# Row maximum of the attention scores through a difference of keys: pairs 0 to 7 beside the MLP, with ScalarE's relu and a fourth PSUM bank

## Chip, cores and metric

One core of one Trainium2 chip runs the whole program. The metric is the device time of one execution in microseconds (us); lower is better. The five engines of the core are called PE (TensorE, matmuls), DVE (VectorE), ACT (ScalarE), POOL (GpSimd) and SP (SyncE, which here only issues DMAs); PEld is PE's weight load. Each engine works through its own instructions in their order.

## The reference

S = 2048 tokens, D = 640 channels, 32 heads of width 20, MLP width F = 1728, all in fp32:

```python
g = sigmoid((x * gate_w).sum(-1, keepdims=True))
q, k, v = heads of x @ wqkv
a = softmax(q @ k.T * 20 ** -0.5) @ v  -> heads joined -> @ wo
h = layernorm(x)                        # over the channels
u = gelu(h.T @ w1 + b1)                 # over the tokens: (D, S) @ (S, F)
b = (u @ w2 + b2).T
out = g * a + (1 - g) * b
```

The softmax is made stable with the maximum of each query's 2048 scores. The change touches how that maximum is found, and when.

## The kernel before

**Layout.** The 32 heads are taken as 16 pairs. fp32 products are made from a rounded part and a rest ("hi" and "lo", helper `hi_lo`): q is stored twice in DRAM (`q_d[0]` hi, `q_d[1]` lo), and so is k (`k_d`). A "stack" of a pair (`load_stack`, L95 on) puts 60 rows per head into one tile: hi, hi and lo of k against hi, lo and hi of q, so that one matmul of 60 rows gives a score tile in full precision. Head j of a pair sits at partition 64 j, so the matmuls of the two heads use different row groups of PE and run beside each other.

**Stages.** First PE makes q, k, v and the gate (`qk_unit`, L213, is one 128x512 piece: 15 matmuls, then ACT takes hi and DVE lo out of PSUM, and two DMAs store them). Then comes the MLP (`mlp`), then the attention loop, then the output projection.

**The maximum pass.** `s_tiles` (L168) makes for each pair, half of the queries, tile t of 128 queries and chunk kc of 512 keys the scores of both heads, j = 1 and then j = 0: one matmul (L178) into a PSUM tile of tag "s" (3 banks, taken in turn), and one DVE `tensor_reduce` with max (L180) of 128x512 into a column of `mx`. That is 128 tiles for a pair and 2048 in all. After each half, `s_max` and `s_store` take the maximum over the four chunks, negate it, split it and store it; the attention loop later loads it as two extra rows of q (`load_m`), so that its own matmul gives score minus maximum.

**Where the pass is put.** The pass is a generator; `s_next` emits one tile. PE's order is written out by hand. In the MLP, every step (`pair64`, L46: two matmuls of 64 rows, one in each row group) is followed by as many pairs of score tiles as an even spread of `S_AHEAD = 736` tiles over all 2592 steps asks for. So 5 pairs and three quarters are done there. The MLP has four PSUM banks of tag "st" of its own, and its results leave PSUM through ACT (L440, L452, L477); ACT also makes the hi parts of weights (L38), and POOL the lo parts (L41). The eighth PSUM bank, tag "pv", is used in the attention loop alone.

**The attention loop** has 512 iterations (16 pairs, 2 halves of the queries, 16 key tiles). Each has four matmuls of scores (L700, tag "st"), four exponentials on ACT (L703, 128x512 each), and eight matmuls with v into the bank "pv" (L637). Between the four score matmuls stand up to three tiles of the maximum pass, spread evenly: `due = (n + 1) * LEFT // 484 + 1` with `LEFT = 2048 - S_AHEAD`, and `take = min(due - given, 3)` in iteration n. With 1312 tiles left this gives 344 iterations with three, 140 with two and the last 28 with none.

**Loading the stacks.** In the MLP the stack of the next pair is put on a list (`drip`) when a pair starts, and one of its DMAs (18 for a pair) is issued on SP's queue at every second opportunity between score tiles. SP's queue carries the MLP's weights, too. The very first stack is loaded by POOL. In the loop, `s_stack` loads pair by pair on SP.

Of the kernel before, what the change touches and what calls it, by code (L numbers as in the profile page):

```python
# [7 lines left out]
F32 = mybir.dt.float32  # L8
F32R = mybir.dt.float32r
AF = mybir.ActivationFunctionType  # L10
OP = mybir.AluOpType
AX = mybir.AxisListType

P = 128
S, D, H, DH, F = 2048, 640, 32, 20, 1728
NP = H // 2
NT = S // P
NC = D // P
FF = 13
FT = 14  # L20
TL = F - FF * P
HALF = D // 2
VW = DH + 1
# [5 lines left out]
def gated_mix(ctx, tc, xT, x, wqk, wv0, wv1, wo, w1, w1t, b1, w2, b2, out):  # L29
    nc = tc.nc  # L30
# [5 lines left out]
    def hi_lo(hi, lo, src, hi_eng=None, lo_eng=None):  # L36
        if hi_eng is nc.scalar:
            nc.scalar.activation(hi, src, AF.Copy)  # L38
        else:
            (hi_eng or nc.vector).tensor_copy(hi, src)  # L40
        (lo_eng or nc.vector).tensor_sub(lo, src, hi.bitcast(F32))  # L41
# [12 lines left out]
    dram = ctx.enter_context(tc.tile_pool(name="dram", bufs=1, space=bass.MemoryType.DRAM))  # L54
    q_d = dram.tile([2, D, S], F32, name="q_d")
    k_d = dram.tile([2, D, S], F32, name="k_d")
    m_d = dram.tile([NP, 2, P, 32], F32, name="m_d")
    o_d = dram.tile([D, S], F32, name="o_d")
    l_d = dram.tile([H, S], F32, name="l_d")
# [4 lines left out]
    cp = ctx.enter_context(tc.tile_pool(name="cp", bufs=1))  # L64
    base = ctx.enter_context(tc.tile_pool(name="base", bufs=1))
    psum = ctx.enter_context(tc.tile_pool(name="psum", bufs=1, space=PSUM))
# [4 lines left out]
    def s_tile(shape, name):  # L71
        return psum.tile(shape, F32, tag="s", bufs=3, name=name)
# [12 lines left out]
    nc.gpsimd.memset(eps_t, EPS)  # L85
    b1_t = cp.tile([P, FT], F32, name="b1_t")
    b2_t = cp.tile([P, NT], F32, name="b2_t")
# [8 lines left out]
    drip = []  # L96

    def load_stack(p, ks, qs, full, eng=nc.sync):
        put = eng.dma_start if eng else lambda *a: drip.append(lambda: nc.sync.dma_start(*a))
        for j in range(2):  # L100
            r0 = 64 * j
            h = 2 * p + j
            rows = slice(DH * h, DH * h + DH)
            kf = ks.bitcast(F32)
            put(kf[r0: r0 + DH, :], k_d[0, rows, :])
            put(kf[r0 + DH: r0 + 2 * DH, :], k_d[0, rows, :])
            put(kf[r0 + 2 * DH: r0 + 3 * DH, :], k_d[1, rows, :])
            if full:
                put(kf[r0 + 3 * DH: r0 + 3 * DH + 2, :], ones)
            for i in range(2):  # L110
                qf = qs[i].bitcast(F32)
                cols = slice(i * (S // 2), (i + 1) * (S // 2))
                put(qf[r0: r0 + DH, :], q_d[0, rows, cols])
                put(qf[r0 + DH: r0 + 2 * DH, :], q_d[1, rows, cols])
                put(qf[r0 + 2 * DH: r0 + 3 * DH, :], q_d[0, rows, cols])
# [15 lines left out]
    s_src, st_src, v_tiles = {}, {}, {}  # L131
# [8 lines left out]
    def s_max(p, half, mx):  # L140
        mm = cp.tile([P, 16], F32, tag="mm", bufs=2, name=f"mm{p}_{half}")
        mc = cp.tile([P, 32], F32R, tag="mc", bufs=2, name=f"mc{p}_{half}")
        nc.vector.tensor_reduce(mm, mx.rearrange("p k j t -> p (j t) k"), axis=AX.X, op=OP.max)
        nc.gpsimd.tensor_scalar_mul(mm, mm, -1.0)
        hi_lo(mc[:, :16], mc[:, 16:], mm, hi_eng=nc.gpsimd, lo_eng=nc.gpsimd)
        s_close.append([8, lambda: s_store(p, half, mc)])
# [16 lines left out]
    def s_finish():  # L163
        next(stream, None)
        while s_close:
            s_close.pop(0)[1]()

    def s_tiles(p):  # L168
        for half in range(2):
            mx = cp.tile([P, 4, 2, 8], F32, tag="mx", bufs=2, name=f"mx{p}_{half}")  # L170
            for t in range(8):
                for kc in range(4):
                    for j in (1, 0):
                        def f(j=j, kc=kc, t=t):
                            ks, qs = s_src[p]
                            ps = s_tile([P, 512], f"s{p}_{half}_{t}_{j}_{kc}")
                            r = slice(64 * j, 64 * j + 3 * DH)
                            nc.tensor.matmul(ps, qs[half][r, t * P:(t + 1) * P], ks[r, kc * 512:(kc + 1) * 512],  # L178
                                             start=True, stop=True)
                            nc.vector.tensor_reduce(mx[:, kc, j, t: t + 1], ps, axis=AX.X, op=OP.max)  # L180
                        yield f
            s_close.append([2, lambda p=p, half=half, mx=mx: s_max(p, half, mx)])

# [10 lines left out]
    p1 = p1s.enter_context(tc.tile_pool(name="p1", bufs=1, side="right"))  # L194
# [13 lines left out]
        hi_lo(wh, wl, raw, hi_eng=nc.scalar)  # L208
        return wh, wl

    accs = iter(range(1000))

    def qk_unit(m, w, q):  # L213
        wh, wl = w
        ps = st_tile([P, 512], f"qk{m}_{q}")
        mm3(ps, [(wh[:, c], wl[:, c], xh[c][q], xl[c][q]) for c in range(NC)])
        hi = p1.tile([P, 512], F32R, tag="evh", bufs=2, name=f"evh{m}_{q}")
        lo = p1.tile([P, 512], F32R, tag="evl", bufs=2, name=f"evl{m}_{q}")
        hi_lo(hi, lo, ps, hi_eng=nc.scalar)
        dst = q_d if m < NC else k_d  # L220
        rows = slice((m % NC) * P, (m % NC + 1) * P)
        cols = slice(q * 512, (q + 1) * 512)
        nc.sync.dma_start(dst[0, rows, cols], hi.bitcast(F32))
        nc.sync.dma_start(dst[1, rows, cols], lo.bitcast(F32))
# [68 lines left out]
    for half in range(2):  # L293
        wvh, wvl = wvs[half]
        width = HALF + 2 if half == 0 else HALF
        for t in range(NT):
            n = NT * half + t
# [9 lines left out]
            ps = st_tile([P, width], f"v{half}_{t}")  # L307
            q, cols = t // 4, slice((t % 4) * P, (t % 4 + 1) * P)
# [47 lines left out]
    for _ in range(2):  # L356
# [3 lines left out]
        for t in range(NT):  # L360
            for c in range(4):
                w_list.append((w2[t][:, 4 * c: min(4 * c + 4, FT)], False))
    AHEAD = 4
# [61 lines left out]
    gps = ExitStack()  # L425
    gp = gps.enter_context(tc.tile_pool(name="gp", bufs=1, side="right"))

    soon = []

    def settle(all_=False):  # L430
# [30 lines left out]
    def u_swap(d, xg):  # L461
        sw = gp.tile([P, HALF], F32, tag="sw", bufs=1, name=f"sw{d}")
        nc.gpsimd.dma_start(sw[:TL], xg[TL:])
        nc.gpsimd.dma_start(sw[TL:], xg[:TL])
        sws.append(sw)

    def u_tail(f, d, xg, gh):
        nc.scalar.activation(xg, xg, AF.Gelu_apprx_tanh, bias=b1_t[:, f:f + 1])
        ht = gp.tile([P, HALF], F32R, tag="ht", bufs=1, name=f"ht{d}")
        nc.gpsimd.tensor_copy(ht[TL:], xg[TL:])  # L470
        nc.gpsimd.tensor_copy(gh[:TL], xg[:TL])
        nc.gpsimd.tensor_sub(gh[TL:], xg[TL:], ht[TL:].bitcast(F32))

# [15 lines left out]
    def mlp(hs):  # L489
        k = 0  # L490
        for d in range(2):
# [16 lines left out]
            for t in range(NT):  # L508
                ps = [st_tile([P, HALF], f"y{d}_{t}_{i}") for i in range(2)]
                for c in range(4):  # L510
                    wh, wl = w_need(k)
                    k += 1
                    for i in range(4 if c < 3 else 2):
# [6 lines left out]
                        else:  # L520
                            nc.tensor.matmul(ps[0], wl[:TL, i], gh[:TL], start=False, stop=False)
                            pair64(ps, wh[:, i], gh, False, True)
# [12 lines left out]
                h_norm(1, NT - 1)  # L535
                hs[NT - 1] = h_split(1, NT - 1)

    S_AHEAD = 736
    STEPS = 2 * ((FT - 1) * 48 + 32 + NT * 40)

    def start_ahead(p):
        if 2 <= p + 1 < 6:
            s_src[p + 1] = base_stack(p + 1, False, None)

    hooks[0] = start_ahead
# [1 line left out]
    done = 0  # L547
    for n, _ in enumerate(steps):
        settle()
        while done + 2 <= S_AHEAD and done < S_AHEAD * (n + 1) / STEPS:  # L550
            if done == 48:
                s_src[1] = base_stack(1, False, None)
            if done == 4 * 128 + 40:
                st_src[0] = base_stack(0, True, None)
                for half in range(2):
                    load_m(0, st_src[0][1], half, lambda *a: drip.append(lambda: nc.sync.dma_start(*a)))
                drip.append(lambda: load_v(0))
            if drip and done % 4 == 0:
                drip.pop(0)()
            for _ in range(2):  # L560
                s_next()
            done += 2
    settle(True)
    while done < S_AHEAD:
        s_next()
# [8 lines left out]
    def s_stack(p):  # L574
        ks = lp.tile([P, S], F32R, tag="sk", bufs=2, name=f"sk{p}")
        qs = [lp.tile([P, S // 2], F32R, tag="sq", bufs=4, name=f"sq{p}_{i}") for i in range(2)]
        load_stack(p, ks, qs, False)
        return ks, qs
# [5 lines left out]

    hooks[0] = start_loop
    M_LAG[0] = 0
    s_src[6] = s_stack(6)

    def norm_steps(h0, h1):
        b = (h1 - h0) * S // P  # L590
# [79 lines left out]
    turn = given = 0  # L670
    LEFT = NP * 128 - S_AHEAD
    for p in range(NP):
        ks, qs = st_src[p]
        if 8 <= p < 8 + NC:
            load_wo(p - 8)
        for it in range(32):
# [10 lines left out]
            if it == 14 and due_stack:  # L687
                n = due_stack.pop()
# [4 lines left out]
            if kt == 0:  # L693
                pv = psum.tile([P, 512], F32, tag="pv", bufs=1, name=f"pv{p}_{qh}")
# [44 lines left out]
    for t in range(NT):  # L739
# [5 lines left out]
        ps = [st_tile([P, HALF], f"a{t}_{i}") for i in range(2)]  # L745
        a_mms(t, ps, o_hl[t // 2], slice((t % 2) * P, (t % 2 + 1) * P), range(NC - 1))
    for t in range(NT):
        ps = [st_tile([P, HALF], f"b{t}_{i}") for i in range(2)]
# [7 lines left out]
def _layout(inputs):  # L756
# [20 lines left out]
        "w1t": c(w1[:, FF * P:].reshape(NT, P, TL).transpose(1, 0, 2)),  # L777
        "b1": c(b1.reshape(FT, P).T),
        "w2": c(w2.reshape(FT, P, NT, P).transpose(2, 1, 0, 3)),
        "b2": c(np.asarray(inputs["B_b2"]).reshape(NT, P).T),  # L780
# [17 lines left out]
```

## Time and profile before

| | us |
|---|---|
| median of 3 runs | 1844.96 (1842.76 to 1847.17) |
| profiled execution, span of the core | 1844.8 |
| q, k, v and gate | 0 to 225.3 |
| MLP with 736 score tiles | 225.3 to 698.4 |
| attention loop with 1312 score tiles | 698.4 to 1705.4 |
| attention loop, last iterations without them | 1705.4 to 1763 |
| output projection | to 1844.8 |

The span is the time from the first to the last instruction of the one profiled execution. The stages are bounded by the first and last matmul of their lines. The page of the profile gives the busy time of each engine, then 40 equal slices of the span with busy tenths; a view by windows gives the same for any stretch, and a timeline gives the instructions with their start times. Instructions of one engine overlap in their records (a DVE instruction of 685 ns is followed by the next one after some 600), so what one costs is read from the distance of two starts, and not from its own length. PE's records overlap even more: two matmuls on different row groups run beside each other, and the next ones are already started.

### The profile page before, as it was taken

To read this page: it belongs to the slowest core of one execution; us is meant where nothing else is said; L and a number is where in the kernel's file an instruction comes from. 1 tells how busy PE (TensorE), PEld (TensorE's weight loads), DVE (VectorE), ACT (ScalarE), POOL (GpSimd) and SP (SyncE) were. 2 spreads that over 40 slices of the span, in tenths; PEclk is the share of its full clock that TensorE was granted. 3 is DMA by queue.
4 is the path that set the end of the run, shared out by engine and by line. 5 is a ranking of instruction groups with operands and counts; after the bars stand their busy time and mean duration, and the time that the engine had idled before them with its cause. 6 is when DMAs were issued, how large, how long until landed. Compare 5 with 4: busy or idle time off the path is not lost. (4 is left out here: it accounts for less than half of the span.)

```text
span 1844.8 us, 39129 instructions
## 1 busy us (share of the span) xinstructions
PE 1829.7 (99%) x14978; PEld 1135.2 (62%) x14978; DVE 1428.9 (77%) x2341; ACT 1361.6 (74%) x2688; POOL 637.1 (35%) x900
## 2 busy tenths in 40 slices
PE   9999999999999999999999999999999999999998
PEld 7998799999999994333333333333333333333378
DVE  4202299999999998888888888888888888888137
ACT  4243244465444448999999999999999999999930
POOL 1013478888887770112112111121321211212210
PEclk9999999999999999999999999999999999999999
DMA  8456766566645645504032324213540423301463
GB/s 289 143 169 212 222 173 173 158 194 193 168 139 166 189 136 121 118 15 103 20 85 61 73 42 93 57 50 78 107 103 24 109 47 77 71 14 23 131 219 132
DMA packets 152831, 216.61 MB, mean 117 GB/s; under 512 B 65698, under 2 KB 92082, under 8 KB 148738
## 3 DMA queue, kind: packets, MB, share of 16 engines
q1 hardware_dynamic: 129172, 178.68, 35.4%
q0 software_dynamic: 14688, 20.78, 5.2%
q10 hardware_dynamic: 8784, 14.65, 2.4%
q8 instruction: 118, 1.93, 0.4%
q14 instruction: 69, 0.57, 0.1%
HBM read 165.43 MB, written 48.25 MB: 116 GB/s over the span
## 5 line engine op out<-in xcount | busy, mean ns | idle before, releaser
L180 DVE TENSOR_REDUCE mx<-s 128x1 f32<-128x512 f32 x2048 | 1293.7, 684 | 159.9 <-PE s L178 119.7
L703 ACT ACTIVATE p<-st 128x512 f32<-128x512 f32 x2048 | 1042.1, 615 | 20.9 <-PE s L178 2.2
L700 PEld LDWEIGHTS st<-qs_True,ks_True 62*128 62x128 f32 x2048 | 307.3, 185 | 485.1 <-ACT p L703 312.9
L700 PE MATMUL st<-qs_True,ks_True 62*128 62x512 f32 x2048 | 579.6, 425 | 0.2 <-ACT ty L477 0.2
L637 PE MATMUL pv<-p,v 128*32 128x512 f32 x4096 | 555.5, 605 | 0.2
L178 PE MATMUL s<-sk,sq 60*128 60x512 f32 x1280 | 423.1, 434 | 0.0
L41 POOL TENSOR_TENSOR wl<-wr,wh 128x512 fp32r<-128x512 f32 x228 | 273.6, 1216 | 59.8 <-ACT wh L38 30.9
L624 POOL DMA_DIRECT2D o_d<-oev x128 | 67.0, 524 | 494.3 <-DVE oev L618 491.6
L178 PE MATMUL s<-ks_False,qs_False 60*128 60x512 f32 x768 | 225.1, 397 | 0.4 <-DVE mx L180 0.3
L46 PE MATMUL y<-gh,wh 64*128 64x320 f32 x896 | 216.8, 308 | 0.0
L46 PE MATMUL y<-gl,wh 64*128 64x320 f32 x832 | 210.3, 306 | 0.0
L46 PE MATMUL y<-gh,wl 64*128 64x320 f32 x832 | 209.4, 305 | 0.0
L38 ACT ACTIVATE wh<-wr 128x512 fp32r<-128x512 f32 (+2 forms) x246 | 135.9, 594 | 90.2 <-PE s L178 29.0
L178 PEld LDWEIGHTS s<-sk,sq 60*128 60x128 f32 x1280 | 197.7, 185 | 1.2
L637 PEld LDWEIGHTS pv<-p,v 128*32 128x32 f32 x4096 | 84.9, 108 | 171.4 <-issue 156.4
L46 PE MATMUL u<-hl,wh 64*128 64x320 f32 x864 | 167.1, 306 | 0.0
L46 PE MATMUL u<-hh,wh 64*128 64x320 f32 x864 | 167.1, 306 | 0.0
L46 PE MATMUL u<-hh,wl 64*128 64x320 f32 x800 | 156.9, 306 | 0.4 <-POOL wl L41 0.4
L46 PEld LDWEIGHTS y<-gh,wh 64*128 64x128 f32 x896 | 155.3, 184 | 0.4
L46 PEld LDWEIGHTS y<-gh,wl 64*128 64x128 f32 x832 | 147.0, 184 | 0.3
L46 PEld LDWEIGHTS y<-gl,wh 64*128 64x128 f32 x832 | 146.9, 184 | 0.0
L178 PEld LDWEIGHTS s<-ks_False,qs_False 60*128 60x128 f32 x768 | 124.4, 184 | 1.1 <-DVE mx L180 1.1
(124 smaller groups left out, 1817.6 us busy)
## 6 DMA issues: line engine op xcount, KB each, us to landing
wr<-in_w_dram SPq DMA_DIRECT2D x196, 256.0 KB
ks_True<-k_d SPq DMA_DIRECT2D x96, 160.0 KB
qs_True<-q_d SPq DMA_DIRECT2D x192, 80.0 KB
sk<-k_d SPq DMA_DIRECT2D x60, 160.0 KB
sq<-q_d SPq DMA_DIRECT2D x120, 80.0 KB
v_d<-vt SPq DMA_DIRECT2D x32, 168.0 KB
v<-v_d SPq DMA_DIRECT2D x16, 336.0 KB
xr<-in_xT_dram SPq DMA_DIRECT2D x20, 256.0 KB
```

The costliest lines, as they stand in the source:

```text
L38: nc.scalar.activation(hi, src, AF.Copy)
L41: (lo_eng or nc.vector).tensor_sub(lo, src, hi.bitcast(F32))
L46: nc.tensor.matmul(ps[k], a[r], b[r], start=start, stop=stop)
L178: nc.tensor.matmul(ps, qs[half][r, t * P:(t + 1) * P], ks[r, kc * 512:(kc + 1) * 512], start=True, stop=True)
L180: nc.vector.tensor_reduce(mx[:, kc, j, t: t + 1], ps, axis=AX.X, op=OP.max)
L624: nc.gpsimd.dma_start(o_d[DH * h: DH * h + DH, cols], ev[r: r + DH, :])
L637: nc.tensor.matmul(pv[r: r + 32, :], v_tiles[p][:, kt, 10 * j: 10 * j + 32], pts[j, c], start=(kt == 0), stop=(kt == NT - 1))
L700: nc.tensor.matmul(ps, ks[r, kt * P:(kt + 1) * P], qs[qh][r, c * 512:(c + 1) * 512], start=True, stop=True)
L703: nc.scalar.activation(pt, ps, AF.Exp, scale=SCALE)
```

## The change

1. **More of the pass beside the MLP.** `S_AHEAD` goes from 736 to 1024: all of pairs 0 to 7 are done beside the MLP, and 1024 tiles are left for the loop.
2. **Two chunks become one maximum for these eight pairs.** With a and b the scores of key chunk 0 and chunk 1, max(a, b) = b + relu(a - b). The stack holds k(chunk 0) - k(chunk 1) in the place of k(chunk 0). For each query tile and head the difference's tile goes to ACT, which writes its relu to SBUF (`over`). Chunk 1's tile goes to a DVE `tensor_tensor_reduce`, which adds `over` and takes the maximum of the sum. Chunks 2 and 3 have a `tensor_reduce` as before. The order of the chunks becomes 0, 2, 1, 3. In the built program the `tensor_tensor_reduce` is two DVE instructions: the main one over 128x512, and one that writes the 128x1 result.
3. **The difference is made in the first stage**: for the three pieces that hold the keys of pairs 0 to 7, `qk_unit` copies chunk 0's tile out of PSUM, subtracts chunk 1's, splits the result into hi and lo and stores both to `kd_d` on POOL's queue.
4. **A fourth bank in the MLP**: every fourth score tile uses the bank "pv".
5. **Loads**: a stack of pairs 0 to 7 has 24 DMAs and not 18 (chunk 0 comes from `kd_d`), and the list is drained at every opportunity. The stacks of pairs 6, 7 and 8 are loaded in the MLP, and the load of pair 6's stack at the loop's start is gone.

```diff
+NDIFF = 8
+DROWS = 3 * 128
+    kd_d = dram.tile([2, DROWS, 512], F32, name="kd_d")
...
-            put(kf[r0: r0 + DH, :], k_d[0, rows, :])
-            put(kf[r0 + DH: r0 + 2 * DH, :], k_d[0, rows, :])
-            put(kf[r0 + 2 * DH: r0 + 3 * DH, :], k_d[1, rows, :])
+            c0 = 0 if full or p >= NDIFF else 512
+            for n, lo in enumerate((0, 0, 1)):
+                r = slice(r0 + n * DH, r0 + (n + 1) * DH)
+                if c0:
+                    put(kf[r, :c0], kd_d[lo, rows, :])
+                put(kf[r, c0:], k_d[lo, rows, c0:])
...
+    def s_mm(p, half, t, j, kc):
+        ks, qs = s_src[p]
+        n = s_count[0]
+        s_count[0] += 1
+        if s_banks[0] == 4 and n % 4 == 3:
+            ps = psum.tile([P, 512], F32, tag="pv", bufs=1, name=f"s{p}_{half}_{t}_{j}_{kc}")
+        else:
+            ps = s_tile([P, 512], f"s{p}_{half}_{t}_{j}_{kc}")
+        r = slice(64 * j, 64 * j + 3 * DH)
+        nc.tensor.matmul(ps, qs[half][r, t * P:(t + 1) * P], ks[r, kc * 512:(kc + 1) * 512], start=True, stop=True)
+        return ps
...
-                for kc in range(4):
+                over = {}
+                for kc in (0, 2, 1, 3) if diff else range(4):
                     for j in (1, 0):
                         def f(j=j, kc=kc, t=t):
...
+                            ps = s_mm(p, half, t, j, kc)
+                            if not diff:
+                                nc.vector.tensor_reduce(mx[:, kc, j, t: t + 1], ps, axis=AX.X, op=OP.max)
+                            elif kc == 0:
+                                over[j] = s_pool[0].tile([P, 512], F32, tag="over", bufs=3, name=f"ov{p}_{half}_{t}_{j}")
+                                nc.scalar.activation(over[j], ps, AF.Relu)
+                            elif kc == 1:
+                                nc.vector.tensor_tensor_reduce(over[j], ps, over[j], 1.0, -3.0e38, OP.add, OP.max,
+                                                               mx[:, 0, j, t: t + 1])
+                            else:
+                                nc.vector.tensor_reduce(mx[:, kc - 1, j, t: t + 1], ps, axis=AX.X, op=OP.max)
...
+        c = m - NC
+        if 0 <= c * P < DROWS and q < 2:
+            if q == 0:
+                k_first[c] = p1.tile([P, 512], F32, tag="kf", bufs=1, name=f"kf{c}")
+                nc.vector.tensor_copy(k_first[c], ps)
+            else:
+                kd = k_first.pop(c)
+                nc.vector.tensor_sub(kd, kd, ps)
+                dh = p1.tile([P, 512], F32R, tag="dh", bufs=1, name=f"dh{c}")
+                hi_lo(dh, kd.bitcast(F32R), kd, hi_eng=nc.scalar)
+                nc.gpsimd.dma_start(kd_d[0, c * P:(c + 1) * P, :], dh.bitcast(F32))
+                nc.gpsimd.dma_start(kd_d[1, c * P:(c + 1) * P, :], kd)
...
-    S_AHEAD = 736
+    S_AHEAD = 1024
...
-        if 2 <= p + 1 < 6:
+        if 2 <= p + 1 < 9:
...
-            if drip and done % 4 == 0:
+            if drip:
...
-    s_src[6] = s_stack(6)
+    s_banks[0] = 3
```

More of the change, by code (lines that the diff above doesn't have):

```diff
@@ L168, in s_tiles @@
+    s_count, s_banks, s_pool = [0], [4], [None]
     def s_tiles(p):
+        diff = p < NDIFF
+        slots = 3 if diff else 4
         for half in range(2):
-            mx = cp.tile([P, 4, 2, 8], F32, tag="mx", bufs=2, name=f"mx{p}_{half}")
+            mx = cp.tile([P, 4, 2, 8], F32, tag="mx", bufs=2, name=f"mx{p}_{half}")[:, :slots]
             for t in range(8):
-                for kc in range(4):
+                over = {}
+                for kc in (0, 2, 1, 3) if diff else range(4):
@@ L173, in s_tiles @@
                     for j in (1, 0):
                         def f(j=j, kc=kc, t=t):
[L175 to L180, printed above, removed]
+                            ps = s_mm(p, half, t, j, kc)
@@ L209, in load_w @@
         return wh, wl
-    accs = iter(range(1000))
+    k_first = {}
     def qk_unit(m, w, q):
@@ L426, in gated_mix @@
     gp = gps.enter_context(tc.tile_pool(name="gp", bufs=1, side="right"))
+    s_pool[0] = gp
     soon = []
```

## The prediction

> **What bounds the kernel now.** I read the page's slices first, then the windows by stage.
>
> ```profile
> span 1844.8 us, 39129 instructions
> ...
> PE   9999999999999999999999999999999999999998
> ...
> DVE  4202299999999998888888888888888888888137
> ACT  4243244465444448999999999999999999999930
> ```
>
> PE is busy everywhere, DVE is at 9 only in the MLP (slices 6 to 15), ACT only in the attention loop. The windows are the MLP, the loop with score tiles, its last iterations, and the rest (columns: window, length, busy us and count of PE, PEld, DVE, ACT, POOL; clock; DMA share; GB/s).
>
> ```profile
> 225.30:698.40 473.10, 472.29 (x5956) 468.51 (x5956) 466.29 (x760) 226.95 (x461) 382.77 (x394) 1.00 0.58 167
> 698.40:1705.40 1007.00, 1006.66 (x7103) 389.49 (x7102) 851.64 (x1388) 986.03 (x1934) 180.59 (x367) 1.00 0.31 68
> 1705.40:1760.00 54.60, 54.48 (x342) 16.38 (x338) 7.17 (x9) 54.50 (x113) 12.56 (x17) 1.00 0.35 111
> ```
>
> A busy PE here only says that its records overlap, so both stages have to be priced from starts. First the MLP, PE's timeline (start, length, line):
>
> ```profile
> 501.28 0.52 PE L178 MATMUL s<-ks_False,qs_False 60*128 60x512 f32 x2
> 501.51 0.44 PE L46 MATMUL u<-hh,wh 64*128 64x320 f32 x2
> ...
> 502.40 0.43 PE L46 MATMUL u<-hh,wh 64*128 64x320 f32 x2
> 502.55 0.52 PE L178 MATMUL s<-ks_False,qs_False 60*128 60x512 f32 x2
> ```
>
> Between the two L46 rows shown lie six MLP steps in 0.89 us: **0.148 us a step**. From one score pair to the next are 1.27 us with seven steps (1.04), so **a score pair costs PE 0.234 us**. Check: 2592 steps and 368 pairs make 383.6 + 86.1 = 470 of the 473.1 us. The MLP is PE's own work.
>
> DVE is close behind. Seven of its reductions in a row, and two neighbours that were not held by PE:
>
> ```profile
> 226.85 4.30 DVE L180 TENSOR_REDUCE mx<-s 128x1 f32<-128x512 f32 x7
> ...
> L180 DVE TENSOR_REDUCE mx<-s 128x1 f32<-128x512 f32 x736 | 463.7, 685 | 5.6 <-PE s L178 1.5
> ...
> L178 PE MATMUL s<-ks_False,qs_False 60*128 60x512 f32 x737 | 213.4, 394 | 0.4 <-DVE mx L180 0.3
> ```
>
> (4.30 - 0.685) / 6 = **0.60 us a reduction**; a pair needs 1.20 of the 1.27 us that PE gives it. PE waits for DVE only 0.4 us in the stage. Now the loop, PE again:
>
> ```profile
> 1307.81 0.49 PE L700 MATMUL st<-qs_True,ks_True 62*128 62x512 f32 x1
> 1307.82 0.72 PE L178 MATMUL s<-sk,sq 60*128 60x512 f32 x2
> ...
> 1308.38 0.39 PE L178 MATMUL s<-sk,sq 60*128 60x512 f32 x1
> ...
> 1308.94 1.07 PE L637 MATMUL pv<-p,v 128*32 128x512 f32 x8
> 1309.93 0.50 PE L700 MATMUL st<-qs_True,ks_True 62*128 62x512 f32 x1
> 1309.94 0.72 PE L178 MATMUL s<-sk,sq 60*128 60x512 f32 x2
> ...
> 1311.83 0.49 PE L700 MATMUL st<-qs_True,ks_True 62*128 62x512 f32 x1
> ```
>
> An iteration with three score tiles takes PE 2.12 us, one with two 1.90. ACT's four exponentials are the other bound; here they run without score tiles:
>
> ```profile
> 1715.65 40.98 ACT L703 ACTIVATE p<-st 128x512 f32<-128x512 f32 x83
> ```
>
> (40.98 - 0.60) / 82 = 0.49 us each, **1.97 us an iteration**. So iterations with three are PE's (2.12), with two ACT's (1.97). Check: 344 x 2.12 + 140 x 1.97 = 1005 of 1007 us.
>
> **The change, part by part.**
>
> *The loop loses 288 score tiles.* With 1024 left, the spread gives 428 iterations with two and 56 with three: 428 x 1.97 + 56 x 2.12 = 962. **Gain 45 us.** No more is to be had, since ACT is late next. The last 28 iterations and the output projection stay.
>
> *The MLP gets 288 tiles.* PE: 144 pairs x 0.234 = **+34 us**, certain, since PE had no idle time to put them in.
>
> *DVE in the MLP.* For each query tile there are eight score tiles (512 pairs, 128 query tiles): two go to ACT, four are reductions, two are the new add-and-maximum. The trace does not show that one. Its nearest rows:
>
> ```profile
> 11.60 3.09 DVE L41 TENSOR_TENSOR xl<-xr,xh 128x512 fp32r<-128x512 f32 x5
> 14.61 0.68 DVE L41 TENSOR_TENSOR evl<-qk,evh 128x512 fp32r<-128x512 f32 x1
> ...
> 515.57 0.26 DVE L143 TENSOR_REDUCE mm<-mx 128x16 f32<-128x64 f32 x1
> 515.74 1.88 DVE L180 TENSOR_REDUCE mx<-s 128x1 f32<-128x512 f32 x3
> ```
>
> Five two-operand instructions over 128x512 take 3.01 us to the next start, 0.60 each, as much as a reduction. The built program has a second instruction behind each, which writes the 128x1 result. The 64-element reduction costs 0.17 from start to start; less its 64 elements at (0.60 - 0.17) / 448 us each, 0.11 is its fixed part. I take 0.10, so **0.70 us** for the two. The ends are 0.60 (the write is hidden) and 0.86 (it waits for the end of the main one's record, 0.685, and takes 0.17). DVE's work for a query tile is 4 x 0.60 + 2 x 0.70 = 3.80 us. PE's is 2592 / 128 = 20.25 steps and four pairs, 3.00 + 0.94 = 3.93.
>
> The Trainium skill (VectorE: DVE Perf Modes, Two Vector instructions with no wait between them) has an op with an accumulator output as two instructions, the main one and a read. By a price of one alone, 0.60, the sum would be 12 us less; no run here has such an op on VectorE yet.
>
> *The ring of four banks.* On average DVE keeps up, but its six tiles come bunched. Counted from the start of tile 2's matmul: its matmul 0.39 (L178's 394 ns) and a hand-over of 0.05 (an estimate, as the restart below), then DVE's 3.80 for tiles 2 to 7, the record's tail 0.685 - 0.60 = 0.08, and PE's restart on the bank. That shows in
>
> ```profile
> 227.58 0.50 PE L178 MATMUL s<-ks_False,qs_False 60*128 60x512 f32 x1 [0.33 <-DVE mx L180]
> ```
>
> 0.05 after the first reduction's end (226.85 + 0.685). So the bank of tile 7 is free after 4.37. The next query tile's tile 3, second of its pair, wants it after 3.93 + 0.12 = 4.05. PE waits, and in order, with the MLP's matmuls behind it. A wait d makes the period longer by d, so that it settles where 4.37 = 4.05 + 2d: d = 0.16, times 128 = **+20 us**. At 0.60 for the new pair of instructions it is 8, at 0.86 it is 41.
>
> *ACT in the MLP.* 256 relus at 0.49 (the exponential's price; also PSUM to SBUF, 128x512) are 125 us more beside 227 in 473: there is room. But a relu now stands in ACT's queue behind the MLP's results and weights, and PE behind the relu's bank. A y tile's end in the first half:
>
> ```profile
> 383.00 0.62 ACT L477 ACTIVATE ty<-y,b2o,omg 128x320 f32<-128x320 f32 x1 [1.30 <-PE y L46]
> ...
> 385.35 0.92 ACT L38 ACTIVATE wh<-wr 128x256 fp32r<-128x256 f32 x2
> ```
>
> That is 3.27 us without a gap. The second relu is done some 1.6 us after its pair's start (0.44 + 2 x 0.49, a tail, a restart) and tile 5 wants the bank at 2.06, so it can come 0.46 late at no cost. Of 16 such blocks about one in four meets a relu, with up to 2.8 us of loss: 16 / 4 x 1.4 = 6. ACT also waits in the stage:
>
> ```profile
> ACT xg L458 <- POOL xg L442: 50.0, 25, 4.0
> ...
> ACT wh L38 <- DMA wr<-in_w_dram: 11.9, 5, 7.3
> ```
>
> Most of these are waits of an ACT that runs ahead; tied to PE by its relus it comes later, and they shrink. I take **+8 us** for ACT together; the ends are 0 and 20.
>
> *First stage.* Nine DVE instructions (5.4 us), three ACT casts and six stores on POOL's queue, in a stage that has
>
> ```profile
> 0.00:225.30 225.30, 219.22 (x1090) 189.46 (x1090) 55.12 (x102) 82.86 (x167) 53.80 (x110) 0.98 0.66 208
> ```
>
> DVE at 55 of 225 us: hidden, but for banks held a little longer, **+1** (0 to 3). If POOL's queue had to wait for the difference, its loads behind would come late; it has 53.8 us of work in 225.3.
>
> *Loads.* A stack of 24 DMAs at one per score pair is out after 24 x 1.0 = 24 us of a pair's 64 x 1.0; three stacks move into the MLP (DMA share 0.58) and 48 small DMAs are added. SP waits for no one there: 0. If a stack's slot came free late, the weights queued behind it on SP would be late, and PE with them; PE's 100% in the stage speaks against that today.
>
> **The sum.** Against the profiled 1844.8 us: +34 + 20 + 8 + 1 - 45 = +18, **1863 us**. The median of the runs shown is 1844.96, so nothing is to be added.
>
> **Rivals.**
>
> *The ring doesn't bite* (faster). If the hand-over is quicker than my bounds or PE fills in with steps while a bank is taken, only PE's own work is left: +34 + 1 - 45 = -10, **1835**. It speaks for it that with three banks and DVE at 95% PE waits 0.4 us now. Against: there the tiles come evenly, two per 1.27 us. It decides where DVE's work for a query tile is below 3.48 us (4.05 = 0.44 + 3.48 + 0.13), or where each wait is under 0.08.
>
> *Half of it* (the same): the second instruction hidden, ring 8, ACT 3: +34 + 8 + 3 + 1 - 45 = +1, **1846**.
>
> *The result's write waits for the main instruction* (0.86): ring 41, sum +39, **1884**. For it: it reads what the main one makes. Against: ordinary neighbours on DVE start 0.08 before the end of the record.
>
> *The new instruction runs at half rate*: 2 x 0.60 + 0.10 = 1.30, DVE needs 5.0 for a query tile and becomes the bound: (5.04 - 3.93) x 128 = 142, sum 34 + 142 + 1 - 45 = +132, **1977**. Against: the two-operand rows at 0.60, with both operands in SBUF and with one in PSUM. The Trainium skill (Vector Engine (DVE) Microarchitecture Reference, 7. Points that are easy to get wrong) says that a scalar-tensor-tensor shape with two non-bf16 SBUF sources runs at half throughput, since no read port is left for the accumulator; here one source is in PSUM, and no run shows the case.
>
> **How the numbers follow.** Forecast (1852 to 1874) 0.50, no ring 0.20, half of it 0.13, late write 0.12, half rate 0.05. A measurement of this kernel can tell about 0.2%, 3.7 us, from no change. Faster is the no-ring case, 0.20; the same is the half case, 0.13; slower is the rest, 0.67. The range takes in the forecast's bounds and all but the half-rate case and the edges of two others: 1833 to 1888.
>
> **What would show it.** In the changed profile: the loop's window some 45 us shorter with ACT at 98% or more; the MLP some 62 us longer; L46 and L178 waiting for DVE in PE's waits, at the second tile of the pair with chunk 2; the new DVE instruction 0.60 apart from its second one and 0.10 behind it. It would be wrong if the loop's iterations with two tiles aren't at 1.97, if no such waits show, or if DVE's six tiles take far from 3.8 us.

## The result and the profile after

The changed kernel takes **1871.55 us** (median of 4 runs, 1871.33 to 1873.55) against 1845.75 us of the kernel before in the same comparison: a ratio of 1.0143, 95% interval 1.0129 to 1.0158. It is slower by 26 us; the profiled executions differ by 1869.4 - 1844.8 = 24.6 us.

The page of the changed kernel, as far as it answers to the lines shown of before:

```profile
span 1869.4 us, 39888 instructions
...
PE   9999899999999999999999999999999999999998
...
DVE  4203288999889999876777777777767777777136
ACT  4353256677766666799999999999999999999920
```

DVE is no longer at 9 all through the MLP, and PE has a slice below 9 at its start (slice 5). ACT went from mostly 4 to 6 or 7 there, and in the loop it stays the bound. The windows, first the MLP and then the loop with score tiles:

```profile
226.00:769.00 543.00, 531.67 (x6242) 512.39 (x6243) 481.08 (x1054) 354.55 (x717) 389.28 (x410) 0.98 0.58 156
769.00:1726.40 957.40, 957.00 (x6816) 363.97 (x6813) 681.40 (x1093) 953.84 (x1934) 174.70 (x350) 1.00 0.31 65
```

Two things are to be seen. In the loop ACT is busy for 953.84 of 957.4 us: 484 iterations at 1.98 us. In the MLP PE's busy share fell below its window, and its granted clock, the third number from the end, is 0.98 and not 1.00. Stage by stage (from the first matmul of a stage to the first of the next):

| us | before | after | |
|---|---|---|---|
| first stage | 225.3 | 226.0 | +0.7 |
| MLP | 473.0 | 543.0 | +70.0 |
| loop, to the first projection matmul | 1065.3 | 1015.7 | -49.6 |
| output projection | 81.3 | 84.8 | +3.5 |

PE's own work in the MLP, by the prices of the prediction, is 470 us before and 2592 x 0.148 + 512 x 0.234 = 503.5 after. So by these prices 39.5 us of the MLP are not PE's work, against 3.2 before. PE's waits in that window (engine, tile, line <- releaser: us, times, longest) tell most of them:

```profile
PEld s L183 <- ACT ov L203: 15.2, 14, 3.8
...
PEld s L183 <- DVE mx L208: 11.6, 53, 0.3
```

The first is rare and long, a wait for ACT's relu; the second is short and frequent, a wait for DVE. The third part is the clock, in windows around the long waits:

```profile
226.00:240.00 14.00, 11.27 (x112) 10.49 (x111) 8.27 (x17) 5.68 (x11) 5.13 (x4) 0.88 0.64 208
274.00:292.00 18.00, 14.43 (x142) 13.55 (x140) 10.76 (x24) 7.35 (x15) 11.87 (x13) 0.81 0.49 121
500.00:510.00 10.00, 6.85 (x62) 6.42 (x60) 4.61 (x10) 7.08 (x15) 6.78 (x10) 0.83 0.80 167
549.00:560.00 11.00, 9.49 (x88) 8.50 (x86) 6.68 (x16) 6.27 (x13) 9.00 (x10) 0.84 0.67 161
560.00:769.00 209.00, 208.82 (x2498) 201.68 (x2496) 191.95 (x423) 131.32 (x263) 145.71 (x152) 1.00 0.51 142
```

In each of the first four PE is idle for 1.5 to 3.6 us, and the clock falls; in the 209 us after them it is 1.00. The trace has the clock at half for 3.4 us (once 6.8), 17.1 us in all. The matmuls that start in these 17.1 us are worth 8.4 us by the plain prices, so that about 8.5 are lost (an estimate, since a small part of it falls into the waits themselves). So 15.2 + 11.6 + 8.5 = 35 of the 39.5 us.

The four long waits have three causes, and ACT's timeline shows them. (The MLP works through the channels in two halves; in each it makes 14 pieces of `u`, with a gelu, and then 16 tiles of `y`.) At the stage's start the first relu writes into a pool whose space is still read by a store of the first stage:

```profile
230.94 1.09 ACT L203 ACTIVATE ov<-s 128x512 f32<-128x512 f32 x2 [3.72 <-DMA k_d<-evl]
```

In both halves ACT stands at the gelu of the tail piece (1728 = 13 x 128 + 64), which waits for POOL's add; the relus are behind it. In the first half POOL waits 3.98 us for the two small DMAs that bring `sw` (in the second the view names another DMA for 1.98 us; which it was isn't settled). The first half, ACT and then POOL:

```profile
280.14 0.56 ACT L509 ACTIVATE xg<-xg,b_t 128x320 f32<-128x320 f32 x1 [6.84 <-POOL xg L486]
280.61 1.06 ACT L203 ACTIVATE ov<-s 128x512 f32<-128x512 f32 x2
```

```profile
279.26 0.85 POOL L486 TENSOR_TENSOR xg<-xg,sw 128x320 f32<-128x320 f32 x1 [3.98 <-DMA sw<-xg]
```

And at the end of the first half ACT does 4.9 us of evacuations, splits, normalisations and a weight's cast in a row before it comes to the relu:

```profile
499.12 0.62 ACT L518 ACTIVATE ty<-y,b2o,omg 128x320 f32<-128x320 f32 x1 [1.08 <-PE s L183]
...
503.51 0.61 ACT L40 ACTIVATE wh<-wr 128x512 fp32r<-128x512 f32 x1
504.03 1.07 ACT L203 ACTIVATE ov<-s 128x512 f32<-128x512 f32 x2
```

The kernel before has the waits at the tail's gelu too, as long as here (11.6 us in two waits in the changed kernel):

```profile
ACT xg L468 <- POOL xg L445: 11.1, 2, 5.6
```

There they cost PE nothing that shows: no wait of PE for ACT stands among its rows in that stage.

### The profile page after: what moved, and what is told of

The parts are those of the page before. It is cut to its first block, busy times and chain, and to the rows that moved or that the text cites. A ratio compares the mean times of both kernels' runs of the same rounds, so it can differ in the third digit from the quotient of the medians.

```text
span 1869.4 us, 39888 instructions
## 1 busy us (share of the span) xinstructions
PE 1840.4 (98%) x14978; PEld 1154.2 (62%) x14978; DVE 1279.5 (68%) x2350; ACT 1459.1 (78%) x2947; POOL 644.2 (34%) x912
## 5 line engine op out<-in xcount | busy, mean ns | idle before, releaser
L200 DVE TENSOR_REDUCE mx<-s 128x1 f32<-128x512 f32 x1024 | 657.9, 685 | 269.9 <-PE s L183 210.2
L741 PE MATMUL st<-qs_True,ks_True 62*128 62x512 f32 x2048 | 530.9, 423 | 0.2 <-ACT ty L518 0.2
L183 PE MATMUL s<-ks_False,qs_False 60*128 60x512 f32 x1152 | 397.0, 413 | 11.3 <-ACT ov L203 11.3
L208 DVE TENSOR_REDUCE mx<-s 128x1 f32<-128x512 f32 x512 | 329.3, 685 | 47.8 <-PE s L183 45.1
L183 PE MATMUL s<-sk,sq 60*128 60x512 f32 x896 | 339.9, 468 | 0.0
L203 ACT ACTIVATE ov<-s 128x512 f32<-128x512 f32 x256 | 138.5, 593 | 119.6 <-PE s L183 115.6
L183 PEld LDWEIGHTS s<-ks_False,qs_False 60*128 60x128 f32 x1152 | 211.9, 186 | 30.4 <-ACT ov L203 15.2
L48 PE MATMUL u<-hh,wh 64*128 64x320 f32 x864 | 217.0, 313 | 0.0
L48 PE MATMUL u<-hl,wh 64*128 64x320 f32 x864 | 216.9, 313 | 0.0
L48 PE MATMUL u<-hh,wl 64*128 64x320 f32 x800 | 203.3, 312 | 0.0
L205 DVE CUSTOM_DVE_ANT_0 ov<-s,ov 128x512 f32<-128x512 f32 x256 | 165.8, 685 | 12.9 <-PE s L183 7.0
```

What stands on the lines that cost most here:

```text
L48: nc.tensor.matmul(ps[k], a[r], b[r], start=start, stop=stop)
L203: nc.scalar.activation(over[j], ps, AF.Relu)
L205: nc.vector.tensor_tensor_reduce(over[j], ps, over[j], 1.0, -3.0e38, OP.add, OP.max, mx[:, 0, j, t: t + 1])
L208: nc.vector.tensor_reduce(mx[:, kc - 1, j, t: t + 1], ps, axis=AX.X, op=OP.max)
L741: nc.tensor.matmul(ps, ks[r, kt * P:(kt + 1) * P], qs[qh][r, c * 512:(c + 1) * 512], start=True, stop=True)
```

## The experiments

Theory after the result: beside PE's own 34 us the MLP loses in ACT's queue (long waits and the half clock behind them, some 20 us) and in the bunching of DVE's six tiles (some 12). Rival: a score pair is dearer on PE in this arrangement, or DVE is the bound, and ACT's waits are incidental. "Before" was 1845.4 to 1846.5 us beside these runs.

**1. unblocked: what stands long ahead of a relu is moved.** `soon` holds what is to be emitted a number of MLP steps later.

```diff
-soon.append([30, lambda: nc.gpsimd.tensor_add(xg, xg, sws.pop())])
-soon.append([44, lambda: u_tail(f, d, xg, gh)])
+soon.append([60, lambda: nc.gpsimd.tensor_add(xg, xg, sws.pop())])
+soon.append([90, lambda: u_tail(f, d, xg, gh)])
...
-hs[NT - 2] = h_split(1, NT - 2)
-h_norm(1, NT - 1)
-hs[NT - 1] = h_split(1, NT - 1)
+def late(t):
+    hs[t] = h_split(1, t)
+soon.append([8, lambda: late(NT - 2)])
+soon.append([16, lambda: h_norm(1, NT - 1)])
+soon.append([24, lambda: late(NT - 1)])
...
-while done + 2 <= S_AHEAD and done < S_AHEAD * (n + 1) / STEPS:
+while done + 2 <= S_AHEAD and done < S_AHEAD * (n - 39) / (STEPS - 40):
```

> As the changed kernel, but nothing that ACT has to wait for long stands ahead of a relu: score tiles begin 40 MLP steps later, the tail piece's add on POOL and its gelu on ACT come 60 and 90 steps after their matmuls (30 and 44 in the changed kernel), and the last two splits of the first half are spread over 24 steps. Theory (of the MLP's 543 us some 20 are four long waits of PE behind a relu, 11.3 us, and the half clock that follows each, 17 us at half rate): MLP about 523, whole 1852 (1848 to 1856), no half clock inside the MLP. Rival (the excess over PE's own 503 us is the ring's waits for DVE and a dearer score pair, the clock is chance): MLP 538 or more, whole 1866 or more.

Measured: 1881.72 us, ratio 1.0188 (1.0173 to 1.0203): slower than the changed kernel. MLP 553.7. The numbers lie in the rival's open range, but its mechanism isn't what the rows show: the waits for DVE fell to 5.3 us. The four long waits and the half clock are gone, as the theory said, but PE waits for a relu at 15 of the first half's 16 y tiles, all but one for 1.2 to 1.5 us, some 20 us together:

```profile
PEld s L183 <- ACT ov L203: 31.1, 44, 1.5
```

In the changed kernel no wait for a relu stands in these y tiles (worked out from the trace). So the place of the score tiles matters: now a pair for the relu comes right at the end of each y tile, behind 3.3 us of ACT work. A y tile is 40 steps, which are 8.03 pairs in this pacing and 7.90 in the changed kernel's. With four pairs to a query tile the place therefore hardly moves from y tile to y tile, and a bad one repeats. (tail_end, below, takes the later start back, and these waits are gone.)

**2. no_relu: ACT taken out of the ring.**

```diff
 elif kc == 0:
-    over[j] = s_pool[0].tile(...)
-    nc.scalar.activation(over[j], ps, AF.Relu)
+    pass
 elif kc == 1:
-    nc.vector.tensor_tensor_reduce(over[j], ps, over[j], ...)
+    nc.vector.tensor_reduce(mx[:, 0, j, t: t + 1], ps, axis=AX.X, op=OP.max)
```

> As the changed kernel, but the relu and the addition are left out: the difference's tile is computed by PE and read by nobody, chunk 1 is reduced alone, so the maximum misses chunk 0. PE's work and DVE's count of instructions per query tile are as in the changed kernel, ACT has no score tiles. Theory (ACT's place in the ring is the largest part of the excess): MLP 512 to 518, so whole 1840 to 1847. Rival (PE's score pairs are dearer in this arrangement, or DVE's ring): MLP 532 or more, whole 1860 or more.

Measured: 1849.92 us in one run, MLP 522.9. Between the two, nearer to the theory: 20 us of the 39.5 go with ACT. Of the 19.4 that are left, 11.4 are in the row "PEld s <- DVE mx" (47 times), and one half clock of 3.4 us costs some 1.7; the rest has no row of its own. Score pairs that are dearer on PE by themselves could be 6 us of the loss at most.

**3. diff_736: the new method with the old number of tiles.**

```diff
-NDIFF = 8
+NDIFF = 5
...
-S_AHEAD = 1024
+S_AHEAD = 736
...
-if 2 <= p + 1 < 9:
+if 2 <= p + 1 < 6:
...
+s_src[6] = s_stack(6)
```

> As the changed kernel, but with the 736 tiles of the kernel before beside the MLP (pairs 0 to 4 with the difference, the rest of them plain, fourth bank kept), and its loop. Theory (relus behind ACT's long waits cost by themselves, at any number of tiles): MLP 473 + about 20, whole 1862 to 1870. Rival (what the MLP loses is PE's own added score pairs alone): MLP 470 to 476, whole 1843 to 1850.

Measured: 1871.31 us, ratio 1.0134 (1.0117 to 1.0150); MLP 492.8, loop 1065.6. As the theory said, a little above its range: the new method costs the MLP 19.8 us with the work of PE unchanged, and PE's waits for the relus are 18.0 us there. That the time equals the changed kernel's is a coincidence of -50 in the loop and +50 in the MLP.

**4. plain_1024: the larger number of tiles with the old method.**

```diff
-NDIFF = 8
+NDIFF = 0
```

> As the changed kernel, but no pair uses the difference: 1024 plain reductions on DVE beside the MLP, four banks. Theory (DVE at 0.605 us a reduction sets the MLP): MLP 620 to 630, whole 1948 to 1960. Rival (PE sets it there too): MLP 505 to 515, whole 1835 to 1845.

Measured: 1942.35 us in one run, MLP 617.0 (0.603 us a reduction), a little under the theory's range. PE waits for DVE at almost every pair (the row is for 226 to 790 us; the stage runs to 840):

```profile
PEld s L183 <- DVE mx L200: 99.7, 416, 0.4
```

Without the relus DVE is the bound; at 1024 tiles they are worth 1942 - 1872 = 71 us.

**5. tail_end: as unblocked, without the later start.** Against unblocked:

```diff
-while done + 2 <= S_AHEAD and done < S_AHEAD * (n - 39) / (STEPS - 40):
+while done + 2 <= S_AHEAD and done < S_AHEAD * (n + 1) / STEPS:
```

> As the changed kernel, with the tail piece's add and gelu 60 and 90 steps after their matmuls and the last two splits of the first half spread over 24 steps, but with score tiles from the first step on as in the changed kernel, so that they stand to the y tiles' ACT work as they do there (one y tile is 40 steps or 7.9 score pairs, so what a relu meets there repeats from y tile to y tile). Theory (three of the four long waits go with the half clock behind them, and no y tile waits): MLP 527 to 531, whole 1855 to 1860. Rival (spreading the splits or moving the tail is what made the y tiles wait): 16 waits of over 1 us in the first half's y tiles, whole 1875 or more.

Measured: 1858.75 us, ratio 1.0070 (1.0055 to 1.0085), MLP 531.7. The theory, the MLP 0.7 above its range: of the three long waits one of 1.4 us is left, the half clock fell from 17.1 to 6.8 us, and no y tile waits. The whole is 12.8 us shorter than the changed kernel, the MLP 11.3; so much those three places cost.

**6. spread: DVE's tiles not in a row.**

```diff
-for kc in (0, 2, 1, 3) if diff else range(4):
-    for j in (1, 0):
+spread = ((0, 1), (2, 0), (2, 1), (3, 0), (1, 1), (0, 0), (3, 1), (1, 0))
+for kc, j in spread if diff else [(kc, j) for kc in range(4) for j in (1, 0)]:
```

> As the changed kernel, with another order of a query tile's eight score tiles: chunk 0 of one head, 2 and 2, 3, 1, then chunk 0 of the other head, 3, 1, so that DVE never has six tiles in a row. Theory (the ring's waits for DVE, 11.6 us, come from the bunching): PE's waits for DVE under 4 us, MLP some 8 us shorter unless the relus, now in two places, meet more of ACT's other work; whole 1860 to 1868. Rival (DVE's mean load sets them): waits for DVE stay at 10 or more, whole 1869 to 1874.

Measured: 1864.33 us, ratio 1.0099 (1.0081 to 1.0116), MLP 532.8, as the theory said. The waits for DVE are gone (0.4 us), and the waits for ACT rose from 15.2 to 20.5, of which 7.8 stand in the y tiles of the first half, where the changed kernel has none:

```profile
PEld s L183 <- ACT ov L204: 20.5, 25, 3.1
```

**7. three_banks: the fourth bank taken away.**

```diff
-s_count, s_banks, s_pool = [0], [4], [None]
+s_count, s_banks, s_pool = [0], [3], [None]
```

> As the changed kernel, with three banks for score tiles in the MLP. Theory (a relu that comes late is met by the fourth bank, and so are DVE's six tiles in a row): a further wait per query tile of 0.3 us or more, MLP 580 or more, whole 1905 or more. Rival (the fourth bank is not needed): whole 1866 to 1880.

Measured: 1919.1 us in one run, MLP 591.8, as the theory said; waits for DVE of 25.3 and 25.1 us at two places up to 790 us. In this order of the tiles the fourth bank is worth 48 us.

**8. smooth_spread: tail_end and spread together, the y tiles' splits and normalisations behind their evacuations, and a later start that catches up.**

```diff
-if t > 1: hs[t - 2] = h_split(1, t - 2)
-if t > 0: h_norm(1, t - 1)
+if t > 1: soon.append([10, lambda t=t: late(t - 2)])
+if t > 0: soon.append([16, lambda t=t: h_norm(1, t - 1)])
...
-done < S_AHEAD * (n + 1) / STEPS
+done < min(S_AHEAD * (n + 1) / STEPS, (n - 27) / 2)
```

> As the changed kernel, with the order of spread, the tail of tail_end, the splits and normalisations of the first half's y tiles 10 and 16 steps behind the y tile's own ACT work, and score tiles from step 28 on, closer together until they have caught up by step 132. Theory (without long waits, blocks and bunching the MLP is PE's own 503 us and a little): MLP 508 to 518, no half clock in it, whole 1834 to 1846. Rival (any relu in ACT's queue costs PE some 20 us, however the work is put): MLP 525 or more, whole 1853 or more.

Measured: 1846.82 us, ratio 1.0005 (0.9994 to 1.0016), MLP 519.9. The whole is just above the theory's range and the MLP 2 us above it. One long wait is left, 4.85 us at the start (a relu behind a weight cast that waits 7.5 us for its load), with 6.8 us at half clock behind it.

**9. smooth2: the start behind those weights.** Against smooth_spread:

```diff
-done < min(S_AHEAD * (n + 1) / STEPS, (n - 27) / 2)
+done < min(S_AHEAD * (n + 1) / STEPS, 0.45 * (n - 57))
```

> As smooth_spread, but score tiles begin at step 58 and catch up slowly (0.45 a step, by step 473), behind the first weights that ACT waits for. Theory (the 4.85 us wait at the stage's start and the 6.8 us at half clock behind it were all that it still lost in one place): MLP 510 to 513, whole 1836 to 1841, faster than the kernel before. Rival (the wait only moves, to another relu behind a weight): MLP 518 or more, whole 1844 or more.

Measured: 1844.11 us, ratio 0.9991 (0.9983 to 1.0000), MLP 516.9. The MLP is between the two, the whole at the edge of the rival's range. The wait shrank to 1.99 + 1.10 us and changed its kind: it is no relu now, but the MLP's own matmuls that wait for the first weights. The clock still halves behind it (6.8 us).

**10. smooth2_gelu: the gelu 24 steps behind its matmuls.** Against smooth2:

```diff
-soon.append([18, lambda: u_gelu(f, xg, gh, gl)])
+soon.append([24, lambda: u_gelu(f, xg, gh, gl)])
```

> As smooth2, with the gelu of every piece 24 steps behind its matmuls and not 18. Theory (ACT's waits for POOL at the gelu, 10.6 us in smooth_spread, stand ahead of relus and cost PE a little): waits at the gelu under 4 us, MLP 1 to 4 us shorter than in smooth2. Rival (they cost PE nothing): the same time as smooth2 within 2 us.

Measured: 1843.70 us, ratio 0.9987 (0.9979 to 0.9995). ACT's waits for POOL at the gelu fell from 8.1 to 0.8 us, and the time is that of smooth2: the rival. Against the kernel before it is the only version that is faster clear of its interval, by some 2 us, which is less than the spread of its own runs (1839.89 to 1846.62).

**11. shifted: tail_end with all score tiles 12 steps later.** Against tail_end:

```diff
-done < S_AHEAD * (n + 1) / STEPS
+done < S_AHEAD * (n - 11) / STEPS
```

> As tail_end, with all score tiles 12 MLP steps later, which is about two of a query tile's four pairs (512 pairs over 2580 steps). Theory (unblocked lost its time because a relu stood right behind the ACT work of each y tile of the first half, by its place alone): some 16 waits of PE for a relu of over 0.9 us, one per y tile; MLP 540 or more, whole 1866 or more. Rival (the later start or its wait did it, the place means nothing): no such waits, MLP 525 to 533, whole 1851 to 1859.

Measured: 1863.66 us in one run, MLP 536.4. Between the two. Nine y tiles in a row of the first half have waits for a relu, but of 0.3 to 0.7 us in each, and the stage's start waits 5.3 us. So the place does bring such waits. Why they are so much longer in unblocked isn't settled; its rhythm of 8.03 pairs to a y tile, which keeps the place fixed, is a guess.

**12. smooth2_bunched: smooth2 in the changed kernel's order of tiles.** Against smooth2:

```diff
-for kc, j in spread if diff else [(kc, j) for kc in range(4) for j in (1, 0)]:
+for kc in (0, 2, 1, 3) if diff else range(4):
+    for j in (1, 0):
```

> As smooth2, with the changed kernel's order of the eight score tiles (DVE's six in a row). Theory (bunching costs its waits for DVE, and with ACT's work spread the relus cost little in either order): waits for DVE 8 to 12 us against next to none, MLP 524 to 530, whole 1851 to 1857. Rival (with ACT out of the way the order means nothing): MLP 515 to 519, whole 1842 to 1846.

Measured: 1862.24 us in one run, MLP 535.2: 18 us more than smooth2, more than the theory's 7 to 13. PE's waits for DVE, against 0.4 us in smooth2:

```profile
PEld s L183 <- DVE mx L208: 15.0, 63, 0.4
```

15 of the 18 us are these; the other 3 were not followed up. So the bunched order costs 18 us here, where ACT's work is spread.

## Why the prediction came out as it did

**Direction and range held**, and most of the parts were named; the forecast of 1863 was 9 us low, because errors of the parts in part cancelled. By its terms:

| us | predicted | measured | from |
|---|---|---|---|
| loop | -45 | -49.6 | 1065.3 to 1015.7 |
| PE's own pairs | +34 | 34 to 37 | plain price; y tiles of smooth2 |
| ring, waits for DVE | +20 | 12 to 14 | wait row; y tiles against smooth2 |
| ACT | +8 | about 24 | 15.2 of waits, 8.5 of half clock |
| first stage | +1 | +0.7 | |
| output projection | 0 | +3.5 | |

The three terms of the MLP are estimates that overlap by a few us; together it grew by 70.0, where 62 were forecast. The 16 y tiles of the first half give two of them, since PE hardly waits there in smooth2: from their first matmul to their last they take 116.6 us in the kernel before, 125.7 in smooth2 and 129.1 in the changed kernel. The step from 116.6 to 125.7, for 35.6 more pairs, is 0.25 us a pair. The step from 125.7 to 129.1, over all 2592 steps, is 14 us for the bunched order.

**The loop** went where it was said to, to ACT's 1.98 us an iteration. It gave 4.6 more than the formula, which charged 2.12 for each of the 56 iterations with three tiles: 484 x 1.98 is the whole loop, so they cost no more than the others. That PE catches up in the iterations with two between them (1.90 against 1.97) would explain it, but wasn't tested.

**The new DVE instruction was priced too high.** I took 0.70 for the two, with 0.60 as the lower end for a hidden write. The timeline of the changed kernel shows the lower end:

```profile
702.50 0.69 DVE L205 CUSTOM_DVE_ANT_0 ov<-s,ov 128x512 f32<-128x512 f32 x1
703.11 0.08 DVE L205 DVE_READ_ACCUMULATOR2_ANT mx<- 128x1 f32 x1
703.11 1.28 DVE L208 TENSOR_REDUCE mx<-s 128x1 f32<-128x512 f32 x2
```

The main one starts, 0.61 later its result is written, and at the same moment the next one starts. So the second instruction is there, as the Trainium skill has it (VectorE: DVE Perf Modes, Two Vector instructions with no wait between them), but it costs nothing that shows here. The half rate of the rival did not come either, with one source in PSUM; no run here has this form with both in SBUF. (By that rival's own terms DVE needs 4 x 0.60 + 2 x 1.30 = 5.00 us and not 5.04, and its sum is 1972 and not 1977.)

**The ring was right in kind and place.** The waits stand before the fourth tile of a query tile, the second of the pair with chunk 2, as said: there PE's distances from start to start are longer than its plain ones by some 7 us in all (worked out from the trace), and in no_relu by some 6, where the distance to the next pair is longer too, by some 5. Spreading the tiles takes them away (experiments 6 and 12), so the bunching is shown to be the cause. The size of +20 came closer than its parts: at the 0.60 to 0.61 that was measured the formula gives 8 or 9 us, less than the 12 to 14, and the price of 0.70 that was too high made up for it. That was luck.

**The step that failed is ACT's, "+8 us; the ends are 0 and 20".** Its first half put 6 us on relus that meet the bursts at the ends of the first half's 16 y tiles. In the changed kernel no wait for a relu stands in these tiles. The four long waits (3.0, 3.8, 3.5 and 1.8 us on PEld), with 12.1 of the 15.2 us, stand at places that were not counted: the stage's start, the two tail pieces and the longer burst that closes the first half. Its second half said of ACT's waits for POOL and for loads that "tied to PE by its relus it comes later, and they shrink". On the whole they did: at the gelu of the other pieces from 50.0 to 17.1 us. But the two at the tail's gelu did not (11.1 before, 11.6 after), since they hang on a DMA and not on how early ACT comes. tail_end shows three of the four places to be worth 11 to 13 us. Such a wait is paid twice, since the clock halves behind it, and the prediction had no term for that 8.5 us. unblocked shows that the bursts of the y tiles can cost 20 us when the pacing puts a relu behind each of them; that the changed kernel's pacing does not was not worked out beforehand.

**The output projection** took 3.5 us more in the profiled execution, and 82.8 to 85.1 us in all the experiments, with 736 tiles as with 1024, against 81.3 in the one profile of the kernel before. The changed kernel has a half clock of 3.4 us in the middle of it, but no_relu and tail_end have none there and take 84.6 and 85.1. The cause stays open.

**Where the gain went.** Moving a score tile out of the loop gives 49.6 / 288 = 0.172 us and costs PE 0.117 in the MLP, so the change could have given 16 us at best. Smoothing ACT's queue, the order of the tiles and their start got back 28 of the 26 + 16, for a net gain of 2.

## What to carry to other kernels

When an engine with slack becomes a consumer in PE's ring of banks, its mean load says little: look in its queue for the longest single waits and the longest blocks of work, since PE can come to stand behind each of them and mostly pays again at half clock when the wait is as long as those here. Two of those that cost stood in the view of the waits before, in a row of only 11.1 us with a longest of 5.6; the row of 50.0 us, 25 waits of 2.0 on average, shrank by itself. Price the two ends of a move by the engine that is the bound at each end (here 0.172 against 0.117 us a tile) before anything else, because that is the most it can give. And if work is bunched in a ring of few banks, try another order as well as another bank: here the bank was worth 48 us in the bunched order, and the order 7 us in the changed kernel and 18 in smooth2. No run had three banks with the spread order.

## What the runs showed of the hardware

- **The clock after a wait of PE.** In the MLPs of the changed kernel and the twelve experiments 19 waits of PE (from the start of one matmul to the start of the next) were over 1.75 us, and behind 17 of them, within 4 us of their end, the granted clock went to half, for 3.4 or 6.8 us; two in diff_736, of 3.8 and 2.3 us, were not followed by it. Of 27 between 1.2 and 1.75 us (17 in unblocked alone) one was. The Trainium skill (TensorE: Matmul & The Clock Gate, Part 1: The HAM clock gate) has a gate that halves the clock after about 3.4 us of idleness and opens after about 3.4 us of work: the lengths of 3.4 and 6.8 us agree with that, but a wait of 1.81 us was enough (at 550.3 us of the changed kernel).
- **An accumulator's read on DVE** costs next to nothing behind a 128x512 instruction: 0.61 us from one start to the next with it, 0.60 without.
- **One exponential of 128x512** takes ACT 0.49 us from start to start, and a relu or a cast from PSUM 0.48 to 0.50; DVE takes 0.60 to 0.61 for a 128x512 reduction, subtraction or sum with a maximum.
